# A gated linear-attention layer and its expert FFN: from a chunk loop with a separate expert stage to a pipeline over 256-token tiles

## The chip, the cores and the metric

The kernel runs on one core of a Trainium2 chip. The metric is device time in microseconds, from the start to the end of one execution. The profile is one execution taken by the hardware profiler; its instruction engines are called PE (TensorE's matmuls), PEld (its weight loads), DVE (VectorE), ACT (ScalarE), POOL (GpSimd) and SP (SyncE, which here only issues DMAs).

## The reference

Attention has 4 batches, 8 heads, 768 steps and head size 48. For each step a complex gate `a = a_re + i a_im` is scaled so that its magnitude is at most 0.999; a complex 48 x 48 state per head is multiplied by the gate (per row d) and gets the outer product of k and v added to its real part; the output is q times the real part of the state:

```python
new_re = ar * S_re - ai * S_im
new_im = ar * S_im + ai * S_re
kv = np.einsum('bhd,bhe->bhde', k[:, :, t], v[:, :, t])
S_re, S_im = (new_re + kv, new_im)
y[:, :, t] = np.einsum('bhd,bhde->bhe', q[:, :, t], S_re)
```

The 3072 output rows of 384 then go through one of 8 experts each, by `domain_id`: `h = maximum(x @ w1[e], 0)`, `out = h @ w2[e]`, with 1024 hidden units. Inputs, weights and output are float32 in HBM.

## The kernel before

Both versions use the same algebra: the logarithm of the gate's magnitude (halved sum of squares, clamped) and its angle are summed over time by matmuls with triangular matrices; `exp` of the summed log-magnitude and `sin`/`cos` of the summed angle scale q and k, so that attention becomes a causal masked product of 96-wide vectors plus a product with the running state.

Before, the work is cut into 6 chunks of 128 steps (`c`, L192), each of the 4 batches (`b`) in it: 24 tiles of [128 steps, 8 heads x 48]. Per tile five loads on SP's queue (L203 to L207, 192-byte pieces), then on POOL a cast of v (L210), three products for the squared magnitude (L214 to L216) and one for `ai * (1/ar)` (L220); DVE takes the reciprocal (L219); ACT takes Arctan (L223), Ln (L241), two Exps (L268, L269) and two Sins (L287, L288). A batch's prefix sums (L249 to L257) add one matmul with a ones matrix for each earlier chunk. DVE reduces the angle to one turn (L272 to L276). POOL and DVE share the products that fill `qcat` and `kcat` (L292 to L304). PE transposes them (L318, L319), ACT and DVE copy the halves out of PSUM (L322, L323), PE forms the scores (L332), DVE masks them (L335), PE forms the outputs and the state's increment (L339 to L344), DVE adds the increment (L348), ACT copies the output to fp16 (L351). POOL then scatters the 128 rows with an indirect DMA to `gl_x_sorted` (L353), 512 slots for each expert, at places computed at the start by a routing stage (L91 to L136).

After all attention comes the expert stage (L360 on). 24 indirect scatters write each slot's token number (L365). 16 passes of 256 slots load the rows, transpose them, run the two matmuls (L413, L423) with Relu on ACT and DVE in turns, copy the result and scatter it to the output by token number (L427). Empty slots carry an index out of bounds and are dropped. Weights come as float32 on SP's queue and are converted by ACT and DVE (L160, L162).

The order on each engine is not the program's. A scheduler lists the instructions at build time: an engine that is free in its estimate takes the ready instruction that stands first in the program. It also places a wait wherever two accesses to a buffer or DRAM tensor may touch, so the scatters into one DRAM tensor follow each other. On the chip each engine then runs its list in order.

Of the kernel before, what the change touches and what calls it, by code (L numbers as in the profile page):

```python
# [10 lines left out]
F32 = mybir.dt.float32  # L11
# [18 lines left out]
ESLOT = 512  # L30
NBLK = B * NCH
# [3 lines left out]
def kernel(  # L35
# [24 lines left out]
    make_upper_triangular(nc, utri16[:, :], val=1.0, diag=True)  # L60
    utri16s = cpool.tile([128, 128], F16, name="utri16s")
    make_upper_triangular(nc, utri16s[:, :], val=1.0, diag=False)
    ones16 = cpool.tile([128, 128], F16, name="ones16")
    nc.gpsimd.memset(ones16[:, :], 1.0)
    maskbf = cpool.tile([128, 128], BF16, name="maskbf")
    make_upper_triangular(nc, maskbf[:, :], val=1.0, diag=True)

    halfpi_col = cpool.tile([128, 1], F32, name="halfpi_col")
    nc.gpsimd.memset(halfpi_col[:, :], PI / 2.0)

    e8 = cpool.tile([128, 8], F32, name="e8")
    nc.gpsimd.iota(e8[:, :], pattern=[[1, 8]], base=0, channel_multiplier=0,
                   allow_small_or_imprecise_dtypes=True)

    tok_i32 = cpool.tile([128, NBLK], I32, name="tok_i32")
    nc.gpsimd.iota(tok_i32[:, :], pattern=[[128, NBLK]], base=0, channel_multiplier=1)

    sent_i32 = cpool.tile([128, NE * ESLOT // 128], I32, name="sent_i32")
    nc.gpsimd.iota(sent_i32[:, :], pattern=[[1, NE * ESLOT // 128]], base=OOB_SENT,
                   channel_multiplier=64)  # L80
    nc.sync.dma_start(out=invs_ap[:, :], in_=sent_i32[:, :])

    zero_f16 = cpool.tile([128, 2 * HD], F16, name="zero_f16")
    nc.gpsimd.memset(zero_f16[:, :], 0.0)
    for e in range(NE):
        nc.scalar.dma_start(out=xs_ap[e * ESLOT + ESLOT // 2:(e + 1) * ESLOT, :],
# [378 lines left out]
```

## Time and profile before

| | |
|---|---|
| runs | 505.60, 507.04, 509.84 us (median 507.04) |
| span of the profiled execution, first to last instruction | 502.4 us (its own time stands nowhere else) |
| PE busy, granted clock over the span | 248.8 us (50%), 0.816 |
| DVE busy | 285.7 us (57%) |
| ACT busy | 266.0 us (53%) |
| POOL busy | 280.8 us (56%) |
| DMA | 61.0 MB, mean 121 GB/s |

Busy time is the union of an engine's instructions. A granted clock of 1.00 is TensorE's level of 2.4 GHz and 0.50 its level of 1.2 GHz; figures between are a stretch's mean over the two. The mean of a group in the list of instructions is the duration from start to end, which includes time in which the instruction is held.

### The profile page before, as it was taken

Reading aid. Unit: us, or ns where it says so; the run is one execution under the profiler, and the core shown is the slowest. Engines: PE = TensorE matmul, PEld = TensorE weight load, DVE = VectorE, ACT = ScalarE, POOL = GpSimd, SP = SyncE. Lnnn points to the kernel's source line nnn. Section 1 sums busy time; section 2 is a strip of 40 time slices with the busy share of each in tenths; the row PEclk is TensorE's granted clock in tenths of the full one; section 3 lists DMA queues with packets and bytes.
Section 4 is the critical chain, followed back from the end, with each engine's and each line's share of the span. In section 5 each row is a group of like instructions: output and inputs, shape, how many; then the busy total and the mean of one; then the engine's idle time right before and its main releaser. Section 6 shows DMA issues by size and latency. Waiting matters only on the chain. (4 is left out here: it accounts for less than half of the span.)

```text
span 502.4 us, 5997 instructions
## 1 busy us (share of the span) xinstructions
PE 248.8 (50%) x2026; PEld 175.0 (35%) x2026; DVE 285.7 (57%) x421; ACT 266.0 (53%) x422; POOL 280.8 (56%) x320
## 2 busy tenths in 40 slices
PE   0010005453215454461576568363669667869980
PEld 0000003342203343251354445252446445546650
DVE  3734275956419999989899996942122222322220
ACT  3155474649136976597488538721254425564440
POOL 3456679884398978949997785841011232232231
PEclk9999999999999665685567557755697878999996
DMA  8965414456544574754535611003967727321210
GB/s 254 281 107 97 80 31 79 90 159 161 94 79 86 106 218 96 196 115 95 113 72 110 130 45 25 16 16 51 386 196 277 277 72 254 121 81 60 70 49 14
DMA packets 153166, 61.01 MB, mean 121 GB/s; under 512 B 134817, under 2 KB 148544, under 8 KB 153136
## 3 DMA queue, kind: packets, MB, share of 16 engines
q1 hardware_dynamic: 148016, 51.96, 42.3%
q0 software_dynamic: 3968, 7.10, 3.9%
q10 hardware_dynamic: 1152, 1.57, 0.8%
q8 instruction: 16, 0.26, 0.2%
q14 instruction: 14, 0.11, 0.1%
HBM read 51.93 MB, written 10.25 MB: 124 GB/s over the span
## 5 line engine op out<-in xcount | busy, mean ns | idle before, releaser
L427 POOL DMA_INDIRECT out_dram<-o_sb,invall x32 | 33.4, 1044 | 114.5 <-ACT o_sb L426 48.7
L418 DVE TENSOR_SCALAR h_sb<-h_ps 128x256 f16<-128x256 f32 x64 | 25.3, 422 | 107.5 <-PE h_ps L413 102.6
L413 PE MATMUL h_ps<-xt,w1t 128*128 128x256 f16 x384 | 62.4, 305 | 18.5 <-ACT xt L405 11.9
L318 PE MATMUL tqk_ps<-ident,qcat 128*128 128x128 bf16 x192 | 41.4, 289 | 40.4 <-DVE kcat_t L323 24.3
L219 DVE RECIPROCAL rec<-art 128x384 f32<-128x384 f32 x24 | 60.9, 2539 | 0.0
L413 PEld LDWEIGHTS <-w1t 128*128 128x128 f16 x384 | 41.6, 109 | 36.7 <-issue 28.4
L423 PE MATMUL o_ps<-w2t,h_sb 128*128 128x384 f16 x256 | 52.6, 338 | 0.0
L319 PE MATMUL tqk_ps<-ident,kcat 128*128 128x128 bf16 x192 | 41.8, 294 | 10.5 <-DVE kcat L304 5.3
L365 POOL DMA_INDIRECT gl_inv_sorted<-tok_i,dest_i x24 | 24.5, 1021 | 36.7 <-DMA gl_inv_sorted<-tok_i,dest_i 26.1
L249 PE MATMUL lm_ps<-lm,utri 128*128 128x384 f16 x24 | 10.9, 455 | 67.7 <-DVE lm L243 67.7
L332 PE MATMUL mt_ps<-qcat_t,kcat_t 96*128 96x128 bf16 x192 | 27.3, 290 | 29.6 <-DVE kcat_t L323 26.5
L322 ACT COPY qcat_t<-tqk_ps 128x512 bf16<-128x512 bf16 x48 | 27.8, 579 | 26.6 <-PE tqk_ps L319 25.6
L323 DVE COPY kcat_t<-tqk_ps 128x512 bf16<-128x512 bf16 x48 | 19.6, 408 | 37.6 <-ACT qcat_t L322 36.2
L353 POOL DMA_INDIRECT gl_x_sorted<-xstage,dest_i x24 | 25.6, 1068 | 24.2 <-ACT xstage L351 17.8
L335 DVE TENSOR_TENSOR mtm<-mt_ps,maskbf 128x512 bf16<-128x512 f32 x48 | 32.4, 676 | 11.4 <-PE mt_ps L332 11.0
L416 ACT ACTIVATE h_sb<-h_ps 128x256 f16<-128x256 f32 x64 | 23.0, 385 | 29.2 <-PE h_ps L413 28.9
L319 PEld LDWEIGHTS <-kcat 128*128 128x128 bf16 x192 | 25.7, 134 | 35.5 <-issue 26.5
L243 DVE TENSOR_SCALAR lm<-lnu 128x384 f16<-128x384 f32 x24 | 20.6, 860 | 29.1 <-ACT lnu L241 29.1
L339 PE MATMUL y_ps<-vt,mtm 128*128 128x48 bf16 x192 | 20.9, 210 | 32.2 <-DVE mtm L335 25.4
L426 ACT COPY o_sb<-o_ps 128x384 f32<-128x384 f32 x32 | 15.2, 478 | 40.5 <-PE o_ps L423 26.7
L241 ACT ACTIVATE lnu<-u 128x384 f32<-128x384 f32 x24 | 12.4, 522 | 40.5 <-POOL u L216 40.3
L318 PEld LDWEIGHTS <-qcat 128*128 128x128 bf16 x192 | 26.2, 137 | 22.1 <-POOL u L214 7.5
(86 smaller groups left out, 769.2 us busy)
## 6 DMA issues: line engine op xcount, KB each, us to landing
wstg<-in_moe_w_dram SPq DMA_DIRECT2D x16, 1536.0 KB, 8.6
qt<-in_q_dram SPq DMA_DIRECT2D x24, 192.0 KB, 4.4
kt<-in_k_dram SPq DMA_DIRECT2D x24, 192.0 KB, 3.3
art<-in_a_re_dram SPq DMA_DIRECT2D x24, 192.0 KB, 5.8
ait<-in_a_im_dram SPq DMA_DIRECT2D x24, 192.0 KB, 3.1
vraw<-in_v_dram SPq DMA_DIRECT2D x24, 192.0 KB, 3.8
xrow<-gl_x_sorted SPq DMA_DIRECT2D x16, 192.0 KB, 2.7
gl_x_sorted<-zero_f ACTq DMA_DIRECT2D x8, 192.0 KB, 5.6
```

The costliest lines, as they stand in the source:

```text
L219: nc.vector.reciprocal(out=rec[:, :], in_=art[:, :, :])
L318: nc.tensor.transpose(out=tqk_ps[:, hi, :], in_=qcat[:, h, :], identity=ident[:, :])
L319: nc.tensor.transpose(out=tqk_ps[:, 4 + hi, :], in_=kcat[:, h, :], identity=ident[:, :])
L322: nc.scalar.copy(out=qcat_t[:, :, :], in_=tqk_ps[:, 0:4, :])
L332: nc.tensor.matmul(out=mt_ps[:, hi, :], lhsT=kcat_t[0:96, hi, :], rhs=qcat_t[0:96, hi, :], start=True, stop=True)
L335: nc.vector.tensor_tensor(out=mtm[:, :, :], in0=mt_ps[:, :, :], in1=maskbf[:, None, :].to_broadcast([128, 4, 128]), op=ALU.mult)
L353: nc.gpsimd.indirect_dma_start(out=xs_ap[:, :], out_offset=bass.IndirectOffsetOnAxis(ap=dest_i32[:, blk:blk + 1], axis=0), in_=xstage[:, : ...
L365: nc.gpsimd.indirect_dma_start(out=invs_ap[:, :], out_offset=bass.IndirectOffsetOnAxis(ap=dest_i32[:, blk:blk + 1], axis=0), in_=tok_i32[: ...
L413: nc.tensor.matmul(out=h_ps[:, sub, :], lhsT=w1t[:, fs, j * 128:(j + 1) * 128], rhs=xt[:, fs, :], start=(fs == 0), stop=(fs == 2))
L418: nc.vector.tensor_scalar(out=h_sb[:, j, :], in0=h_ps[:, sub, :], scalar1=0.0, scalar2=None, op0=ALU.max)
L423: nc.tensor.matmul(out=o_ps[:, :], lhsT=h_sb[:, j, th * 128:(th + 1) * 128], rhs=w2t[:, j, :], start=(j == 0), stop=(j == 7))
L427: nc.gpsimd.indirect_dma_start(out=out[:, :], out_offset=bass.IndirectOffsetOnAxis(ap=invall[:, eb * 2 + th:eb * 2 + th + 1], axis=0), in_ ...
```

## The change

The kernel body is rewritten. A tile is 256 steps of one batch, two neighbouring steps in one partition: [128, 8 heads, 2 x 48], 12 tiles, batch after batch, in groups `[[0], [1,2], [3,4,5], [6,7,8], [9,10,11]]`. Loads have pieces of 384 bytes. Gate work is split into a block of Ln/Exp/Square (`le_block`) and a block of Arctan/Sin (`trig_block`), each behind one explicit table load, and ScalarE's order within and between them is fixed (`chain`). `ai / ar` is `ai * Exp(-Ln(ar))`, and the log-magnitude is `2 Ln(ar) + Ln(1 + x*x)`. POOL keeps the cast of v and the DMA issues. All transposed copies go through VectorE. Each tile's output is stored by SP in token order, and an expert call gathers its rows by token number, at most 128 per batch and expert, in slots `rank * 8 + expert`; what does not fit would go through a loop under a run-time test (`overflow`). For this input the largest count is 116. Weights are converted by DMAs from POOL's queue and stay in SBUF. The expert calls of a batch are emitted between the attention tiles of the next batch. Output scatters and inverse scatters are declared free of each other (`unordered`).

```diff
+TS = 256
+CAP = 128
+GROUPS = [[0], [1, 2], [3, 4, 5], [6, 7, 8], [9, 10, 11]]
...
+    pt = pool("pt", 1, space=bass.MemoryType.PSUM)
+    pe = pool("pe", 2, space=bass.MemoryType.PSUM)
...
+    def load(g, names):
+        for name, t in names:
+            bufs = {"ar": 3, "ai": 4, "q": 2, "k": 2, "v": 1}[name]
+            tl = lpool.tile([128, H, 96], F32, name=f"ld_{name}", tag=f"ld_{name}", bufs=bufs)
+            nc.sync.dma_start(out=tl[:, :, :], in_=src_view(t, g))
+            loaded[name, g] = tl
...
+    def load_weights(e, gate):
+        i1 = nc.gpsimd.dma_start(out=w1t[e][:, :, :], in_=moe_w1[e].rearrange("(fs p) f -> p fs f", p=128))
+        i2 = nc.gpsimd.dma_start(out=w2t[e][:, :, :], in_=moe_w2[e].rearrange("(j p) f -> p j f", p=128))
+        for i in (i1, i2):
+            if gate is not None:
+                tc.add_manual_dep(i.ins, gate.ins.name, syncdep, reason="inputs first")
...
+    def le_a(g):
+        ar, ai = loaded["ar", g], loaded["ai", g]
+        la = epool.tile([128, H, 96], F32, name="la")
+        first = chain("act", nc.scalar.activation(out=flat(la), in_=flat(ar), func=AF.Ln))
+        chain("act", nc.scalar.activation(out=flat(ar), in_=flat(la), func=AF.Exp, scale=-1.0))
+        nc.vector.tensor_tensor(out=flat(ai), in0=flat(ai), in1=flat(ar), op=ALU.mult)
+        return la, first
+    def le_b(g, la):
+        ar, ai = loaded["ar", g], loaded["ai", g]
+        nc.scalar.activation(out=flat(ar), in_=flat(ai), func=AF.Square)
+        chain("act", nc.scalar.activation(out=flat(ar), in_=flat(ar), func=AF.Ln, bias=1.0))
+        nc.vector.scalar_tensor_tensor(out=flat(la), in0=flat(la), scalar=2.0, in1=flat(ar),
+                                       op0=ALU.mult, op1=ALU.add)
+        lmt = epool.tile([128, 2, HD], F16, name="lm", bufs=3)
+        nc.vector.tensor_scalar(out=hdx(lmt[:, :, :]), in0=jhd(la[:, :, :]), scalar1=LN0999_X2, scalar2=None,
+                                op0=ALU.min)
+        lm[g] = lmt
+    def le_c(g):
+        ps = pcum.tile([128, 2, 512], F32, name="cum", tag="cum")
+        cumsum(ps, lm, g)
+        for dst, name, sgn, bias in ((ep, "ep", 0.5, bias_p), (em, "em", -0.5, bias_m)):
+            t = epool.tile([128, 2, HD], BF16, name=name, bufs=3)
+            chain("act", nc.scalar.activation(out=t[:, :, :], in_=ps[:, :, 0:HD], func=AF.Exp, scale=sgn,
+                                              bias=bias[:, 0:1]))
+            dst[g] = t
+    def trig_a(g):
+        ai = loaded["ai", g]
+        chain("act", nc.scalar.activation(out=flat(ai), in_=flat(ai), func=AF.Arctan))
+        tht = epool.tile([128, 2, HD], F16, name="th", bufs=3)
+        nc.vector.tensor_scalar(out=hdx(tht[:, :, :]), in0=jhd(ai[:, :, :]),
+                                scalar1=1.0 / (2 * PI), scalar2=None, op0=ALU.mult)
+        th[g] = tht
+    def trig_b(g):
+        ps = pcum.tile([128, 2, 512], F32, name="cum", tag="cum")
+        cumsum(ps, th, g)
+        src = ps[:, :, 0:HD]
+        fg = epool.tile([128, 2, 2, HD], F32, name="fg", bufs=1)
+        nc.vector.tensor_scalar(out=fg[:, 1], in0=src, scalar1=MAGIC, scalar2=None, op0=ALU.add)
+        nc.vector.scalar_tensor_tensor(out=fg[:, 0], in0=fg[:, 1], scalar=MAGIC, in1=src,
+                                       op0=ALU.subtract, op1=ALU.subtract)
+        nc.vector.tensor_scalar(out=fg[:, 1].bitcast(I32), in0=fg[:, 0].bitcast(I32), scalar1=0x7FFFFFFF,
+                                scalar2=None, op0=ALU.bitwise_and)
+        t = epool.tile([128, 2, 2, HD], BF16, name="sc", bufs=2)
+        chain("act", nc.scalar.activation(out=t[:, 0], in_=fg[:, 0], func=AF.Sin, scale=-2 * PI))
+        chain("act", nc.scalar.activation(out=t[:, 1], in_=fg[:, 1], func=AF.Sin, scale=-2 * PI,
+                                          bias=halfpi[:, 0:1]))
+        sc[g] = t
...
+    def attend(g):
+        b, i = divmod(g, NT)
+        vt = epool.tile([128, H, 96], BF16, name="vt", bufs=2)
+        nc.gpsimd.tensor_copy(out=vt[:, :, :], in_=loaded["v", g][:, :, :])
+        v4 = vt[:, :, :].rearrange("p h (j d) -> p h j d", j=2)
+        cats = []
+        for name, e in (("k", em), ("q", ep)):
+            p = e[g]
+            nc.vector.tensor_tensor(out=hdx(p[:, :, :]), in0=jhd(loaded[name, g][:, :, :]), in1=hdx(p[:, :, :]),
+                                    op=ALU.mult)
+            cat = epool.tile([128, 2, H, 2, D], BF16, name=f"{name}cat", bufs=1)
+            for part, s in ((0, 1), (1, 0)):
+                nc.vector.tensor_tensor(
+                    out=cat[:, :, :, part, :].rearrange("p j h d -> p (j h) d"),
+                    in0=p[:, :, :].rearrange("p j (h d) -> p (j h) d", h=H),
+                    in1=sc[g][:, s].rearrange("p j (h d) -> p (j h) d", h=H), op=ALU.mult)
+            cats.append(cat)
+        kcat, qcat = cats
+        if i < NT - 1:
+            w_ps = py.tile([128, HD], F32, name="w_ps", tag="y")
+            for h in range(H):
+                for j in range(2):
+                    chain("pe_y", nc.tensor.matmul(
+                        out=w_ps[0:96, h * D:(h + 1) * D], lhsT=kcat[:, j, h].rearrange("p a d -> p (a d)"),
+                        rhs=v4[:, h, j, :], start=(j == 0), stop=(j == 1)))
+            wn = epool.tile([96, HD], BF16, name="wst", bufs=2)
+            if i == 0:
+                nc.vector.tensor_copy(out=wn[:, :], in_=w_ps[0:96, :])
+                nc.vector.tensor_tensor(out=wn[:, :], in0=wst[g - 1][:, :], in1=w_ps[0:96, :], op=ALU.add)
+            wst[g] = wn
+        xst = mpool.tile([128, 2, HD], F16, name="xst", bufs=2)
+        for hq in range(2):
+            y = py.tile([128, 4, 2, D], F32, name="y", tag="y")
+            for hp in range(2):
+                t_ps = pt.tile([128, 2, 2, 2, 128], BF16, name="t_ps", tag="t")
+                for kind, cat in ((0, qcat), (1, kcat)):
+                    for hh in range(2):
+                        for j in range(2):
+                            h = hq * 4 + hp * 2 + hh
+                            nc.tensor.transpose(out=t_ps[0:96, kind, hh, j, :],
+                                                in_=cat[:, j, h].rearrange("p a d -> p (a d)"),
+                                                identity=ident[:, :])
+                ct = epool.tile([96, 2, 2, 2, 128], BF16, name="ct", bufs=2)
+                nc.vector.tensor_copy(out=ct[:, :, :, :, :], in_=t_ps[0:96])
+                for hh in range(2):
+                    h = hq * 4 + hp * 2 + hh
+                    mt = pm.tile([128, 2, 256], F32, name="mt", tag="mt")
+                    for js in range(2):
+                        nc.tensor.matmul(out=mt[:, js, :], lhsT=ct[:, 1, hh, js, :],
+                                         rhs=ct[:, 0, hh].rearrange("p j t -> p (j t)"), start=True, stop=True)
+                    mtm = epool.tile([128, 2, 2, 128], BF16, name="mtm", bufs=3)
+                    nc.vector.tensor_tensor(out=mtm[:, :, :, :].rearrange("p a b t -> p (a b t)"),
+                                            in0=mt[:, :, :].rearrange("p a t -> p (a t)"),
+                                            in1=mask[:, :, :, :].rearrange("p a b t -> p (a b t)"), op=ALU.mult)
+                    for jt in range(2):
+                        o = y[:, hp * 2 + hh, jt, :]
+                        for js in range(2):
+                            chain("pe_y", nc.tensor.matmul(out=o, lhsT=mtm[:, js, jt, :], rhs=v4[:, h, js, :],
+                                                           start=(js == 0), stop=(i == 0 and js == 1)))
+                        if i > 0:
+                            chain("pe_y", nc.tensor.matmul(out=o, lhsT=ct[:, 0, hh, jt, :],
+                                                           rhs=wst[g - 1][:, h * D:(h + 1) * D],
+                                                           start=False, stop=True))
+            nc.scalar.copy(
+                out=xst[:, :, hq * 4 * D:(hq + 1) * 4 * D].rearrange("p j (h d) -> p h j d", d=D), in_=y[:, :, :, :])
+        nc.sync.dma_start(out=x_ap[b][i * TS:(i + 1) * TS, :].rearrange("(p j) f -> p j f", j=2), in_=xst[:, :, :])
...
+    def gather(b, n, idx):
+        x = xrow[n % XSLOTS]
+        nc.gpsimd.indirect_dma_start(
+            out=x[:, :], out_offset=None, in_=x_ap[b][:, :],
+            in_offset=bass.IndirectOffsetOnAxis(ap=idx, axis=0), bounds_check=S - 1, oob_is_err=False)
+        return x
+    def ffn(x, w1, w2, inv, group=None):
+        xt_ps = pe.tile([128, 3, 128], F16, name="xt_ps", tag="moe")
+        for fs in range(3):
+            nc.tensor.transpose(out=xt_ps[:, fs, :], in_=x[:, fs * 128:(fs + 1) * 128], identity=ident16[:, :])
+        xt = mpool.tile([128, 3, 128], F16, name="xt", bufs=2)
+        nc.vector.tensor_copy(out=xt[:, :, :], in_=xt_ps[:, :, :])
+        h_sb = mpool.tile([128, 8, 128], F16, name="h_sb", bufs=2)
+        for half in range(2):
+            h_ps = pe.tile([128, 4, 128], F32, name="h_ps", tag="moe")
+            for jj in range(4):
+                j = half * 4 + jj
+                for fs in range(3):
+                    nc.tensor.matmul(out=h_ps[:, jj, :], lhsT=w1[:, fs, j * 128:(j + 1) * 128],
+                                     rhs=xt[:, fs, :], start=(fs == 0), stop=(fs == 2))
+            nc.scalar.activation(out=h_sb[:, half * 4:half * 4 + 4, :], in_=h_ps[:, :, :], func=AF.Relu)
+        o_ps = pe.tile([128, HD], F32, name="o_ps", tag="moe")
+        for j in range(8):
+            nc.tensor.matmul(out=o_ps[:, :], lhsT=h_sb[:, j, :], rhs=w2[:, j, :], start=(j == 0), stop=(j == 7))
+        o_sb = mpool.tile([128, HD], F32, name="o_sb", bufs=2)
+        nc.scalar.copy(out=o_sb[:, :], in_=o_ps[:, :])
+        ins = nc.gpsimd.indirect_dma_start(
+            out=out[:, :], out_offset=bass.IndirectOffsetOnAxis(ap=inv, axis=0), in_=o_sb[:, :],
+            in_offset=None, bounds_check=NTOK - 1, oob_is_err=False)
+        if group:
+            unordered(group, ins)
+    def expert(b, e):
+        x = gather(b, b * NE + e, loc_sb[b][:, e:e + 1])
+        ffn(x, w1t[e], w2t[e], inv_sb[b][:, e:e + 1], group="out")
+    preload = lambda name: chain("act", nc.scalar.preload_act_table_set(name))
+    def le_block(tiles):
+        gates = []
+        preload(SET_LE)
+        las = {}
+        for n, g in enumerate(tiles):
+            las[g], f = le_a(g)
+            gates.append(f)
+            if n > 0:
+                le_b(tiles[n - 1], las[tiles[n - 1]])
+                if n > 1:
+                    le_c(tiles[n - 2])
+        le_b(tiles[-1], las[tiles[-1]])
+        for g in tiles[-2:]:
+            le_c(g)
+        return gates
+    def trig_block(tiles):
+        preload(SET_TRIG)
+        for n, g in enumerate(tiles):
+            trig_a(g)
+            if n > 0:
+                trig_b(tiles[n - 1])
+        trig_b(tiles[-1])
+    load(0, QKV)
+    le_block(GROUPS[0])
+    routing()
+    trig_block(GROUPS[0])
+    gates = {}
+    ffn_todo = []
+    def some_ffn(n):
+        for _ in range(min(n, len(ffn_todo))):
+            expert(*ffn_todo.pop(0))
+    for gi, tiles in enumerate(GROUPS):
+        nxt = GROUPS[gi + 1] if gi + 1 < len(GROUPS) else []
+        for n in nxt:
+            load(n, ARI)
+        if nxt:
+            for n in nxt:
+                load(n, QKV)
+            for n, f in zip(nxt, le_block(nxt)):
+                gates[n] = f
+                if n - 1 < NE:
+                    load_weights(n - 1, f)
+        for n, g in enumerate(tiles):
+            attend(g)
+            if n == 0 and nxt:
+                trig_block(nxt)
+            if g == 0:
+                for b in range(B):
+                    scatter_inverse(b)
+                for b in range(B):
+                    load_inverse(b)
+            some_ffn(3 if g < 10 else 4)
+            if g % NT == NT - 1:
+                ffn_todo += [(g // NT, e) for e in range(NE)]
+    some_ffn(99)
...
+    def overflow():
+        count = nc.values_load(ovf_i[0:1, 0:1], min_val=0, max_val=S)
+        with tc.If(count > CAP):
```

## Rows read from the trace of the kernel before

**Rows 1.** Busy time by stage: us from start, length, busy (instructions) of each engine.
```profile
core 0: us, PE busy (x) PEld busy (x) DVE busy (x) ACT busy (x) POOL busy (x), PEclk, DMA share, GB/s
0.00:24.00 24.00, 0.48 (x2) 0.21 (x2) 13.21 (x43) 5.41 (x4) 8.77 (x30) 1.00 1.00 274
180.00:300.00 120.00, 62.66 (x586) 45.54 (x585) 113.94 (x135) 80.02 (x121) 99.94 (x108) 0.61 0.52 117
...
340.00:502.00 162.00, 112.03 (x774) 75.98 (x771) 36.04 (x73) 65.39 (x137) 35.33 (x34) 0.84 0.45 148
```

**Rows 2.** The page's first part: busy us, share of the span, instructions.
```profile
PE 248.8 (50%) x2026; PEld 175.0 (35%) x2026; DVE 285.7 (57%) x421; ACT 266.0 (53%) x422; POOL 280.8 (56%) x320
```

**Rows 3.** Timeline: start us, duration us, engine, line; VectorE and POOL around 203 us.
```profile
202.88 5.45 DVE L243 TENSOR_SCALAR lm<-lnu 128x384 f16<-128x384 f32 x1
203.52 1.00 POOL L216 TENSOR_TENSOR u<-u,u 128x384 f32<-128x384 f32 x1
...
208.01 1.00 POOL L215 TENSOR_TENSOR u<-art 128x384 f32<-128x384 f32 x1
```

**Rows 4.** Timeline of VectorE and POOL around 319 us.
```profile
319.31 0.34 DVE L273 TENSOR_SCALAR t_s<-t_s 128x384 f32<-128x384 f32 x1
319.39 1.65 POOL L353 DMA_INDIRECT gl_x_sorted<-xstage,dest_i  x1 [0.16 <-issue]
319.58 0.54 DVE L276 SCALAR_TENSOR_TENSOR t_c<-t_s 128x384 f32<-128x384 f32 x1
...
320.51 0.34 DVE L304 TENSOR_TENSOR kcat<-p,sn 128x384 bf16<-128x384 bf16 x1
```

**Rows 5.** Instruction groups of VectorE: shapes, count | busy us, mean ns | idle before.
```profile
L219 DVE RECIPROCAL rec<-art 128x384 f32<-128x384 f32 x24 | 60.9, 2539 | 0.0
L335 DVE TENSOR_TENSOR mtm<-mt_ps,maskbf 128x512 bf16<-128x512 f32 x48 | 32.4, 676 | 11.4 <-PE mt_ps L332 11.0 <-issue 0.3
L304 DVE TENSOR_TENSOR kcat<-p,sn 128x384 bf16<-128x384 bf16 x24 | 23.2, 968 | 0.2 <-PE tcat_ps L344 0.2
L323 DVE COPY kcat_t<-tqk_ps 128x512 bf16<-128x512 bf16 x48 | 19.6, 408 | 37.6 <-ACT qcat_t L322 36.2 <-ACT xstage L351 1.3
L272 DVE TENSOR_SCALAR t_s<-th_ps 128x384 f32<-128x384 f32 x24 | 13.0, 544 | 2.8 <-PE th_ps L254 2.8
```

**Rows 6.** Instruction groups of ScalarE.
```profile
L241 ACT ACT_TABLE_LOAD x22 | 28.2, 1283 | 7.9 <-DMA gl_x_sorted<-zero_f 7.6
L322 ACT COPY qcat_t<-tqk_ps 128x512 bf16<-128x512 bf16 x48 | 27.8, 579 | 26.6 <-PE tqk_ps L319 25.6 <-PE y_ps L341 0.9
L241 ACT ACTIVATE lnu<-u 128x384 f32<-128x384 f32 x24 | 12.4, 522 | 40.5 <-POOL u L216 40.3
L162 ACT CAST w1t<-wstg 128x3072 f16<-128x3072 f32 x4 | 11.0, 2748 | 8.2 <-DMA wstg<-in_moe_w_dram 7.1 <-PE h_ps L413 1.2
L162 ACT ACT_TABLE_LOAD x1 | 1.3, 1283 | 0.7 <-PEq L449 0.7
```

**Rows 7.** PE: two transposes of the timeline; a run of matmuls in the chain of waits.
```profile
241.04 0.31 PE L318 MATMUL tqk_ps<-ident,qcat 128*128 128x128 bf16 x1
241.14 0.31 PE L319 MATMUL tqk_ps<-ident,kcat 128*128 128x128 bf16 x1
...
413.10 2.11 PE o_ps L423 x13
```

**Rows 8.** Instruction groups of POOL.
```profile
L427 POOL DMA_INDIRECT out_dram<-o_sb,invall x32 | 33.4, 1044 | 114.5 <-ACT o_sb L426 48.7 <-DMA out_dram<-o_sb,invall 29.4 <-ACT h_sb L416 26.8
L353 POOL DMA_INDIRECT gl_x_sorted<-xstage,dest_i x24 | 25.6, 1068 | 24.2 <-ACT xstage L351 17.8 <-DVE t_s L272 2.5 <-ACT qcat_t L322 2.0
L210 POOL CAST vt<-vraw 128x384 bf16<-128x384 f32 x24 | 13.2, 550 | 12.1 <-PE y_ps L341 11.7 <-ACT lnu L241 0.3
```

**Rows 9.** The chain of waits near its end: start us, us, what.
```profile
460.80 2.58 DMA out_dram<-o_sb,invall
```

More of the change, by code (lines that the diff above doesn't have):

```diff
@@ L61, with after, chain @@
-    utri16s = cpool.tile([128, 128], F16, name="utri16s")
-    make_upper_triangular(nc, utri16s[:, :], val=1.0, diag=False)
+    nosync = mybir.DependencyInfo(mybir.DependencyClass.NoSync, mybir.DependencyReason.DATA)
+    syncdep = mybir.DependencyInfo(mybir.DependencyClass.Sync, mybir.DependencyReason.DATA)
+    def after(ins, prev):
+        if prev is not None:
+            tc.add_manual_dep(ins.ins, prev.ins.name, nosync, reason="order")
+        return ins
+    last = {}
+    def chain(key, ins):
+        after(ins, last.get(key))
+        last[key] = ins
+        return ins
@@ new lines, in unordered @@
+    def unordered(group, ins):
+        tc.declare_no_dep(ins.ins, group=group, reason="rows written are disjoint")
+        tc.add_to_no_dep_group(group, ins.ins)
+        return ins
+    x_ap = [nc.dram_tensor(f"gl_x_rows{b}", [S, HD], F16, kind="Internal").ap() for b in range(B)]
+    inv_ap = [nc.dram_tensor(f"gl_inv_rows{b}", [NROWS, 1], I32, kind="Internal").ap() for b in range(B)]
+    pool = lambda name, bufs=1, **kw: ctx.enter_context(tc.tile_pool(name=name, bufs=bufs, **kw))
+    cpool = pool("cpool")
@@ L72 @@
[L72 to L81, printed above, removed]
@@ L139 @@
+    mask = cpool.tile([128, 2, 2, 128], BF16, name="mask")
+    for js in range(2):
+        for jt in range(2):
+            nc.vector.tensor_copy(out=mask[:, js, jt, :], in_=(u_str if js > jt else u_inc)[:, :])
     ident = cpool.tile([128, 128], BF16, name="ident")
@@ new lines @@
+    w1t = [cpool.tile([128, 3, DFF], F16, name=f"w1t{e}") for e in range(NE)]
+    w2t = [cpool.tile([128, 8, HD], F16, name=f"w2t{e}") for e in range(NE)]
+    def load_weights(e, gate):
[4 more added lines that the diff above has]
+                tc.add_manual_dep(i.ins, gate.ins.name, syncdep, reason="inputs first")
@@ new lines, with flat, jhd, hdx @@
+    lm = {}
+    th = {}
+    ep = {}
+    em = {}
+    sc = {}
+    def flat(t):
+        return t[:, :, :].rearrange("p h x -> p (h x)")
+    def jhd(ap):
+        return ap.rearrange("p h (j d) -> p j h d", j=2)
+    def hdx(ap):
+        return ap.rearrange("p j (h d) -> p j h d", h=H)
+    def cumsum(ps, tiles, g):
+        b, i = divmod(g, NT)
+        prev = [tiles[b * NT + n] for n in range(i)]
+        cur = tiles[g]
+        for j in range(2):
+            o = ps[:, j, 0:HD]
+            mm = [((u_str if j == 0 else u_inc), cur[:, 1, :]), (u_inc, cur[:, 0, :])]
+            for p in prev:
+                mm += [(ones16, p[:, 0, :]), (ones16, p[:, 1, :])]
+            mm = mm[::-1]
+            for n, (l, r) in enumerate(mm):
+                nc.tensor.matmul(out=o, lhsT=l[:, :], rhs=r, start=(n == 0), stop=(n == len(mm) - 1))
@@ L438 @@
+    overflow()
 _INS = ['q', 'k', 'v', 'a_re', 'a_im', 'moe_domain_id', 'moe_w1', 'moe_w2']
```

440 lines of the change are left out of this document (121 added, 319 removed).

## The prediction

> **What bounds the kernel now.** I read the busy time by stage first [rows 1]. Attention fills 0 to 340 us, the experts 340 to 502. Between 180 and 300 us VectorE is busy 113.9 of 120 us and POOL 99.9, while PE works 62.7 us at a granted clock of 0.61: the attention stage is bound by VectorE. No engine is over 57% over the span [rows 2].
>
> Then the timeline, for what a VectorE instruction costs. L243 takes 5.45 us at 202.88, and in that time POOL runs elementwise work back to back, from 203.52 to past 208.01 [rows 3]. At 319.31 the only POOL instruction is a scatter's issue; beside it a 384-element L273 takes 0.34 us, L276 0.54, L304 0.34 [rows 4]. L304's mean is 968 ns [rows 5]. So POOL's arithmetic, not its DMA issues, doubles these VectorE instructions.
>
> The expert stage is held by neither: in the chain of waits, 2.58 us landings of the output scatter follow each other, one scatter waiting for the last [rows 9], and PE is busy 112 of 162 us at 0.84 [rows 1].
>
> **The change, part by part.** I price the new work per 256-token tile (12 of them) and per expert call (32, of 128 slots).
>
> *VectorE.* Full rate: 544 ns for 384 elements, 676 for 512 [rows 5], so 1.03 ns an element and 0.94 us for 768. Double rate: 0.34 against 0.54 us for 384 [rows 4], half the slope, 0.54 us for 768; a 1024-element bf16 copy from PSUM is 0.41 + 512 x 0.52 ns = 0.675 [L323, rows 5]. Gate work of a tile: four instructions at 0.94 and three at 0.54, 5.4 us. Attention of a tile: two products at 0.94, four bf16 products at 0.54, four copies at 0.675, eight maskings at 0.676, a state update of 0.54 in two tiles of three: 12.5 us. That is 17.9 x 12 = 215; with 32 copies of 0.34 (11) and routing (some 7, from 13.2 busy in the first 24 us [rows 1] less a reciprocal and weight copies) 233 us, against 285.7 [rows 2]. The reciprocal, 60.9 us [rows 5], is gone: Exp(-Ln) on ScalarE replaces it. The seven double-rate instructions of a tile read or write pieces of 48 elements; at full rate they add 7 x 0.4 x 12 = 34 us, at best nothing changes. I take the double rate, since L304 writes such pieces at 0.34.
>
> *ScalarE.* 0.52 us for 384, slope (2748-522)/2688 = 0.83 ns [rows 6], 0.84 for 768. Nine per tile and two copies of 0.52: 8.6 x 12 = 103. An expert call: two Relus of 512 at 0.58 and a copy of 0.52: 54 in all. Table loads fall from 70 (seven rows, first and last in [rows 6]) at 1.28 us to about 11: 14 for 90. Sum 171 for 266. Off the path.
>
> *PE.* I count columns. Transposes follow each other at 0.10 us for 128 columns [rows 7], which is 1.2 GHz; 13 matmuls of 384 took 2.11 us, 0.162 each, which is 2.4 GHz. A batch has 48 prefix matmuls of 384, 96 transposes, 48 score products of 256, 128 output and 32 state products of 48: 50 thousand columns (32 without the prefix sums). An expert call has 27 x 128 + 8 x 384 = 6.5 thousand; eight make 52. All four batches: 410 thousand, 342 us at 1.2 GHz, 171 at 2.4. The change doubles the score columns and leaves the rest near what it was. This is the second bound: where experts stand beside attention, PE has 102 thousand columns a batch, 43 to 86 us, against VectorE's 3 x 17.9 + 2.7 = 56.
>
> *POOL.* All elementwise work goes but 12 casts (0.55 at 384 [rows 8], about 1.0 each). Indirect transfers: 24 inverse scatters, 32 gathers, 32 output scatters at 1.07 [rows 8]: 94. The 16 converting weight loads have no row before. Low end: 1.07 each, 17 us. High end by pieces: L353 writes 128 rows in 1.07, a pair of weight tensors has 384 + 1024 row pieces, 11.8 us an expert, 94 in all. I take the high end, since every piece needs its address: POOL 200 us, under VectorE. They stand on POOL's queue ahead of the inverse scatters and the casts of V that tiles 1 and 2 wait for; cover is the first 90 us, where POOL has little else.
>
> *Waits taken away and added.* The output scatters no longer wait for each other; 162 us of expert stage goes beside attention except for the last batch. Rows no longer reach DRAM sorted: each tile is stored by SP, and a gather fetches an expert's rows; the store waits behind loads on SP. New waits: eight gathers wait for the last tile of their batch; ep and em have three buffers, so the gate work of a batch ends only after the last cat product of the batch before, and the sines follow. That leaves VectorE the rest of one attention (8.5 us) to cover a table load, Arctan, prefix sum, rounding and two sines (about 9): a few us lost at each batch border.
>
> **The sum.** Start: first loads 0.8 MB at 274 GB/s [rows 1] and a 2.6 us landing, 5.5; the gate chain of tile 0 (eleven ScalarE passes and table loads, six VectorE passes, two prefix sums) about 18: 24 us, with 15 us of VectorE work in it. Tiles 0 to 2: 3 x 12.5 + 5 x 5.4 = 64 us of VectorE, at 85% busy 75. Batches 1 and 2: 56 us of VectorE and the border, with PE near 57 at a mean clock of 0.75, 66 each. Batch 3 has no gate work left: VectorE 40, PE 84 thousand columns, 35 to 70; I take 50. Tail: eight expert calls with nothing beside them. A call is 6.5 thousand columns, 2.7 us at 2.4 GHz, and the two PSUM buffers it shares among four uses expose Relu and copy, so about 4; 32 plus store, gather and last scatter at 2.6 and 1.1 each, 42 us. Then the overflow test, some 3 us (no row; 0 to 8). The largest count of a batch and expert is 116, below 128, so its body is skipped. 24 + 75 + 132 + 50 + 42 + 3 = 326; 80% of the middle is VectorE-busy, less than the 95% of [rows 1], because two engines compete. With 4.6 us around the span (median 507.04 less span 502.4, the profile giving no other time for its execution) 331; I say **334**, for waits in queues ordered at build time by estimates.
>
> **Rivals.**
> - *PE stays at half clock beside attention.* For it: 0.61 with PE busy 63 of 120 us. Against: 0.84 in the expert stage, where it is busy 112 of 162 [rows 1], and the new stage is denser than the old attention. At 1.2 GHz batches 1 and 2 take 86/0.95 = 90 each, batch 3 74, the tail 58: 334 + 48 + 24 + 16 = 422; half of that 378. Chance 0.15.
> - *POOL's queue starves the early tiles.* If five experts' weights and the 24 inverse scatters (59 + 26 us) go ahead of the casts of V, attention of tile 1 starts near 90 us instead of 42 and VectorE has only gate work of tiles up to 5 for that time: +35, 370. Against: the cheap end of the weight price. Chance 0.17.
> - *VectorE's locks stretch POOL's DMA issues until POOL is the bound*, slower than before. For it: L353 takes 1.65 us beside three such VectorE instructions [rows 4], 1.07 on average [rows 8]. Against: L427, in the stage with little VectorE work, averages 1.04. The place is POOL's 200 us; it decides from a factor of 2.5, where POOL alone takes 500. At three, with start and end, 620. At the 1.65 shown, 200 becomes 310, still covered. Chance 0.04. The Trainium skill's rule speaks for it ("SBUF — State Buffer", SBUF: two separate sides: a VectorE instruction that uses both ports keeps POOL from writing descriptors); its estimate of 620 ns becoming 3100 would put POOL near 1000 us, and no row here shows more than 1.65.
> - *Less idle than I allow*: VectorE at 92% through the middle, PE at full clock, tail of 34: 24 + 213/0.92 + 34 + 8 = 298. Chance 0.09.
>
> That the change does not do what it says would be expert calls ordered behind attention: 24 x 4 = +96 less the PE time freed beside attention, about 400; I hold it inside the first rival's chance.
>
> **The numbers.** Forecast case 305 to 360 with the rest, 0.55. The range 302 to 400 leaves out most of the low case and the upper half of the PE case and the slow one, about 0.18; the double-rate question (+34) lies inside. Within 1% (what a measurement of this kernel can tell; its runs lie within 0.8%): 0.02. Slower 0.04. Faster 0.94.
>
> **What would show it.** Right: VectorE's 768-element products near 0.54 and 0.94 us with means near their minima; VectorE 225 to 245 us busy; 11 table loads; expert matmuls between 120 us and the end, with 8 calls alone at the end over 35 to 45 us. Wrong: PE clock under 0.65 between 100 and 250 us; POOL busy throughout the first 100 us with VectorE idle behind a cast; POOL issues over 2 us; VectorE 270 or more.

## The result and the profile after

The changed kernel takes **385.64 us** (median of 4 runs, 385.29 to 387.06), the kernel before 506.32 beside it: ratio 0.761, 95% interval 0.758 to 0.764. The forecast was 334 us, the range 302 to 400: direction and range held, the point was 52 us too low.

Windows of the kernel after (busy us by engine, granted clock, share of the 16 DMA engines, GB/s), against [rows 1]:

```profile
22.00:57.00 35.00, 16.41 (x121) 11.08 (x122) 19.00 (x31) 15.69 (x19) 22.76 (x21) 0.78 0.66 75
57.00:190.00 133.00, 67.34 (x548) 45.73 (x546) 73.32 (x112) 48.66 (x64) 30.69 (x32) 0.62 1.01 195
190.00:335.00 145.00, 124.77 (x1571) 94.23 (x1571) 110.34 (x184) 74.83 (x122) 48.02 (x44) 0.99 0.24 72
335.00:384.00 49.00, 27.34 (x280) 19.50 (x280) 2.86 (x8) 13.52 (x25) 17.04 (x17) 0.85 0.14 46
```

From 57 to 190 us the DMA share averages 1.01, and every compute engine is busy about half the time or less. The share sums the time of all packets, so it passes 1 where they overlap, and a mean near 1 can hide a hole. Finer windows show two, in which the DMA engines stand nearly idle, and a long full stretch:

```profile
24.00:40.00 16.00, 11.87 (x94) 8.56 (x92) 11.95 (x18) 10.50 (x14) 12.95 (x12) 1.00 0.09 5
64.00:80.00 16.00, 0.00 (x0) 0.00 (x0) 0.59 (x2) 0.00 (x0) 3.73 (x4) 0.50 0.29 37
80.00:190.00 110.00, 66.60 (x545) 45.68 (x545) 71.77 (x110) 48.66 (x64) 25.02 (x26) 0.65 1.10 217
```

From 190 to 335 us PE works 125 of 145 us at a granted clock of 0.99. Batch ends are read from SP's stores of a tile; here the last tiles of batches 0 to 2, and one row for the three of batch 3 (the last at 335.16):

```profile
139.68 0.52 SPq L372 DMA_DIRECT2D gl_x_rows<-xst  x1
...
222.57 0.34 SPq L372 DMA_DIRECT2D gl_x_rows<-xst  x1
...
284.09 0.34 SPq L372 DMA_DIRECT2D gl_x_rows<-xst  x1
302.14 33.33 SPq L372 DMA_DIRECT2D gl_x_rows<-xst  x3
```

Stage lengths, with two experiments for later:

| us | forecast | after | one weight (e3) | one weight, lookup moved (e11) |
|---|---|---|---|---|
| start to end of batch 0 | 99 | 139.7 | 130.2 | 113.0 |
| batch 1 | 66 | 82.9 | 63.5 | 62.4 |
| batch 2 | 66 | 61.5 | 65.6 | 67.9 |
| batch 3 | 50 | 51.1 | 49.4 | 58.8 |
| tail, overflow test | 45 | 48.9 | 52.3 | 53.5 |

The miss is 40.7 + 16.9 before 223 us; the later stages add 0.5 net (-4.5 + 1.1 + 3.9), and 1.5 us outside the span for 4.6 takes 3 off, and the 3 us for waits that the forecast had beyond its sum take off as many. The busy sums, against [rows 2], and groups of VectorE and POOL (shapes, count, busy us, mean ns, idle before), against [rows 5, 8]:

```profile
PE 240.1 (63%) x2530; PEld 171.9 (45%) x2530; DVE 217.5 (57%) x374; ACT 162.2 (42%) x238; POOL 126.1 (33%) x139
```
```profile
L358 DVE TENSOR_TENSOR mtm<-mt,mask 128x512 bf16<-128x512 f32 x96 | 63.0, 683 | 8.2 <-PE mt L355 7.9
L316 DVE TENSOR_TENSOR kcat<-em,sc 128x768 bf16<-128x768 bf16 x24 | 14.3, 599 | 0.5 <-ACT sc L296 0.5
L312 DVE TENSOR_TENSOR em<-ld_k,em 128x768 bf16<-128x768 f32 x12 | 11.3, 946 | 7.5 <-DMA ld_k<-in_k_dram 7.5
...
L199 POOL DMA_INDIRECT gl_inv_rows<-tok_i,dest_i x24 | 26.7, 1111 | 32.3 <-DMA w2t<-in_moe_w_dram 8.8 <-DMA w1t<-in_moe_w_dram 6.9 <-DMA ld_k<-in_k_dram 6.6
L215 POOL DMA_DIRECT2D w2t<-in_moe_w_dram x8 | 7.4, 925 | 0.0
L214 POOL DMA_DIRECT2D w1t<-in_moe_w_dram x8 | 6.2, 774 | 21.6 <-ACT la L252 21.6
```

L316 works on 768 elements in 599 ns, where L304 of [rows 5] took 968 for 384. The weight loads cost POOL 13.6 us in all, under the low end of the price (17). Ahead of the inverse scatters, though, POOL stood idle for 32.3 us, half of it behind weight transfers. What that does, in VectorE's and POOL's timelines (the bracket is the idle time before, and its releaser):

```profile
51.73 0.17 DVE L206 TENSOR_SCALAR loc_sb<-inv_sb 128x8 int32<-128x8 int32 x1 [14.01 <-DMA inv_sb<-gl_inv_rows]
79.41 0.17 DVE L206 TENSOR_SCALAR loc_sb<-inv_sb 128x8 int32<-128x8 int32 x1 [20.68 <-DMA inv_sb<-gl_inv_rows]
...
178.92 0.36 DVE L387 COPY xt<-xt_ps 128x384 f16<-128x384 f16 x1 [13.62 <-PE xt_ps L385]
```
```profile
73.73 0.97 POOL L199 DMA_INDIRECT gl_inv_rows<-tok_i,dest_i  x1 [0.30 <-issue]
74.70 0.83 POOL L307 CAST vt<-ld_v 128x768 bf16<-128x768 f32 x1
```

VectorE stands 35 us at two subtractions of 8 columns. At 178.92 it waits for the first expert's rows, whose gather was issued at 154.42 behind weight loads and landed 23.92 us later (chain of waits); the gather at 338.03 lands in 2.60. This wait (13.62 us) and the one at the next call (3.00) are nearly all of the 16.9 us that batch 1 is over its forecast. The cast of V for tile 1 is right behind the 24th inverse scatter.

### The profile page after: what moved, and what is told of

It is laid out like the page before. It is cut to its first block, busy times and chain, and to the rows that moved or that the text cites. A ratio compares the mean times of both kernels' runs of the same rounds, so it can differ in the third digit from the quotient of the medians.

```text
span 384.1 us, 6354 instructions
## 1 busy us (share of the span) xinstructions
PE 240.1 (63%) x2530; PEld 171.9 (45%) x2530; DVE 217.5 (57%) x374; ACT 162.2 (42%) x238; POOL 126.1 (33%) x139
## 4 chain that ended last, share of the span: by engine, by line
DMA 29%; PE 22%; DVE 22%; issue 10%; ACT 7%; POOL 6%; POOLq 0%; SPq 0%; DVEq 0%; ACTq 0%
DMA gl_inv_rows<-tok_i,dest_i 9%; DMA xrow<-gl_x_rows,loc_sb 8%; DMA ld_k<-in_k_dram 7%; PE h_ps L394 6%; PE o_ps L399 6%; DVE mtm L358 6%; POOL gl_inv_rows L199 3%; PE cum L247 3%; PE mt L355 3%; DVE ct L350 3%; POOL out_dram L402 2%; DVE fg L290 2%; DVE fg L291 2%; DMA inv_sb<-gl_inv_rows 2%; ACT h_sb L396 2%
## 5 line engine op out<-in xcount | busy, mean ns | idle before, releaser
L358 DVE TENSOR_TENSOR mtm<-mt,mask 128x512 bf16<-128x512 f32 x96 | 63.0, 683 | 8.2 <-PE mt L355 7.9
L396 ACT ACTIVATE h_sb<-h_ps 128x512 f16<-128x512 f32 x64 | 37.7, 595 | 70.4 <-PE h_ps L394 70.0
L402 POOL DMA_INDIRECT out_dram<-o_sb,inv_sb x32 | 34.8, 1088 | 80.5 <-ACT o_sb L401 76.6
L394 PE MATMUL h_ps<-xt,w1t 128*128 128x128 f16 x768 | 56.2, 226 | 5.0 <-DVE xt L387 4.8
L377 POOL DMA_INDIRECT xrow<-gl_x_rows,loc_sb x32 | 35.8, 1119 | 34.5 <-PE xt_ps L385 9.8
L355 PE MATMUL mt<-ct 96*128 96x256 bf16 x192 | 34.3, 307 | 15.3 <-DVE ct L350 15.2
L364 PE MATMUL y<-vt,mtm 128*128 128x48 bf16 x384 | 29.1, 194 | 23.4 <-DVE mtm L358 22.9
L350 DVE COPY ct<-t_ps 96x1024 bf16<-96x1024 bf16 x48 | 32.6, 679 | 16.9 <-PE t_ps L346 16.8
L364 PEld LDWEIGHTS <-mtm 128*128 128x128 bf16 x384 | 22.1, 104 | 36.2 <-DVE mtm L358 32.1
L199 POOL DMA_INDIRECT gl_inv_rows<-tok_i,dest_i x24 | 26.7, 1111 | 32.3 <-DMA w2t<-in_moe_w_dram 8.8
L247 PEld LDWEIGHTS <-ones 128*128 128x128 f16 x96 | 10.9, 119 | 52.3 <-DVE fg L291 37.2
```

The lines of the kernel that those rows point to most:

```text
L199: unordered(f"inv{b}", nc.gpsimd.indirect_dma_start(out=inv_ap[b][:, :], out_offset=bass.IndirectOffsetOnAxis(ap=dest_i[:, col:col + 1], a ...
L247: nc.tensor.matmul(out=o, lhsT=l[:, :], rhs=r, start=(n == 0), stop=(n == len(mm) - 1))
L350: nc.vector.tensor_copy(out=ct[:, :, :, :, :], in_=t_ps[0:96])
L355: nc.tensor.matmul(out=mt[:, js, :], lhsT=ct[:, 1, hh, js, :], rhs=ct[:, 0, hh].rearrange("p j t -> p (j t)"), start=True, stop=True)
L358: nc.vector.tensor_tensor(out=mtm[:, :, :, :].rearrange("p a b t -> p (a b t)"), in0=mt[:, :, :].rearrange("p a t -> p (a t)"), in1=mask[: ...
L364: chain("pe_y", nc.tensor.matmul(out=o, lhsT=mtm[:, js, jt, :], rhs=v4[:, h, js, :], start=(js == 0), stop=(i == 0 and js == 1)))
```

## The experiments

Theory: the 57 us before 223 are a term that the sum lacked, the DMA engines' time for 25.2 MB of f32 weights beside the inputs (the profile books them at their f16 size, 12.6 MB). Rival: the order of the queues alone. For the later stages: PE is full, so expert calls beside attention are not free.

**Order of the queues (e1, e2, e8).** e1 puts the subtraction behind the last masking of its batch; e2 puts all inverse scatters ahead of the weights:

```
 e1   def local_rows(b):
+         after(nc.vector.tensor_scalar(out=loc_sb[b]..., last["dve"])
 e2   for i in (i1, i2):
+         after(i, last["inv"])
```


> Only VectorE's order changes: the four lookups that wait for the inverse scatters stand behind the last masking of their batch instead of in tile 1. Theory A (VectorE stands in its queue behind small transfers that are late): the two waits of 14.0 and 20.7 us go; but POOL's cast of V for tile 1 still stands behind the last inverse scatter at 73.7 us, so only part comes back: 360 to 372 us. Theory B (from 25 to 175 us the kernel is bound by what the DMA engines can move, and the wait only shows it): no change, 380 to 387.

> All 24 inverse scatters stand on POOL's queue ahead of the first weight load. Theory A: the scatters end near 46 us instead of 73.7, the lookups wait until about 55 us, the cast of V is free too; the late k load (7.5 us) and the late gather (13.6 us) stay: 350 to 362 us. Theory B: the same bytes must move, 380 to 387.

e1: 391.11 us (ratio 0.765, 0.754 to 0.777), e2: 386.65 (0.757, 0.751 to 0.762): no gain. In e1 VectorE does 25.2 us of work from 22 to 57 us instead of 19.0, then stands 25.2 us at a state update that needs the cast of V: the next wait takes the place of the one removed. e2 leaves the DMA engines idle early and full later (the rows are e2's windows), and ends where the kernel after does.

```profile
22.00:57.00 35.00, 16.06 (x108) 10.54 (x108) 16.55 (x26) 15.29 (x18) 28.41 (x27) 0.80 0.20 17
57.00:190.00 133.00, 66.21 (x553) 45.77 (x554) 76.45 (x117) 48.62 (x64) 25.66 (x26) 0.64 1.09 210
```

e8 sends only batch 0's inverse scatters early, each later batch's behind a cast of V, with e1's edit:

```
-            if g == 0:
-                for b in range(B):
...
+            if g == 0 or (g % NT == NT - 1 and g // NT + 1 < B):
+                b = 0 if g == 0 else g // NT + 1
```


> All weights. Only batch 0's six inverse scatters come early; those of each later batch stand behind the casts of V of the batch before, and each lookup behind its batch's last masking. So the first weights are issued near 27 us instead of 39.7, and no cast or load waits for 24 scatters. Theory B: the gain is the DMA time no longer idle between 22 and 57 us, about 15 us: 365 to 375. Theory A alone (queue order): 345 to 355. No change would speak against both.

397.69 us (0.778, 0.770 to 0.786), slower. The DMA share is 1.03 at 161 GB/s from 22 to 57 us, then 0.97 at 177, and by 190 us VectorE has done 111 us of work, 104 in the kernel after. But the gathers in batch 1 stand behind weight loads as before, and VectorE waits 17.18 and 8.31 us at copies of their rows, the first of them here:

```profile
165.40 0.36 DVE L392 COPY xt<-xt_ps 128x384 f16<-128x384 f16 x1 [17.18 <-PE xt_ps L390]
```

Batch 2 then takes 70.6 us for 61.5. Pulling the weights forward as well, seven experts' ahead of the first gather, gave 394.10 us (0.771, 0.761 to 0.780; e9). That gather lands in 5.28 us and batch 1 takes 69.0 us, but VectorE waits 22.71 us for a load of k at 127.14: the weights now delay an input. So the place of the weights decided which transfer was late. e8 came out in none of its cases, e9 within 4 us of e8.

**Take the bytes away (e3).** All experts use expert 0's weights, so only those are loaded and the output differs:

```
-                if n - 1 < NE:
+                if n - 1 < 1:
```


> Only expert 0's weights are loaded and all experts compute with them (the output is that of other weights). 11 MB of converting loads go; all work of the engines stays. Theory A: the waits for lookups, k and gather (56 us) go nearly all: 328 to 340 us, what was forecast for the change. Theory B says the same number but with the input loads landing faster everywhere; the difference to the runs before tells them apart: if B, e1 and e2 stay near 385 and this falls. If PE's half clock up to 175 us is the cause (theory C), this stays above 365.

360.84 us (0.706, 0.696 to 0.716): 25 us gone, the one early edit that gains by itself. The DMA share from 57 to 190 falls from 1.01 to 0.58, VectorE does 101 us of work there instead of 73, and batch 1 takes 63.5 us. Two of VectorE's waits in the kernel after are gone with the weights, 13.62 us for the first gather and 7.52 us for a load of k: 21 of the 25 us. This edit takes away the bytes and their place ahead of the gathers on POOL's queue together. No run kept all weights and took their loads off the gathers' queue, so the two are not separated.

**Bytes and queues (e7, e10, e11).** e7 is e1 + e2 + e3. e10 moves the lookups of the inverse table from SP's queue to POOL's behind the scatters, with e1 + e2; e11 is e10 with one weight:

```
-        nc.sync.dma_start(out=inv_sb[b]...
+        nc.gpsimd.dma_start(out=inv_sb[b]...
```


> Expert 0's weights serve all experts (the output is that of other weights), and besides the inverse scatters stand ahead of the weight load and the lookups behind each batch's last masking. The two edits that gave nothing with all weights are put on the kernel that has little weight traffic. Theory B (the DMA engines are saturated from 57 to 190 us, and that hides what the order costs): now the order counts, the 33.6 us of lookup waits left in the run with one weight go: 328 to 340 us, the forecast. Theory D (order and bytes both do not matter, PE's half clock sets the pace): no change, 358 to 362.

> The four lookups of the inverse table leave SP's queue for POOL's, behind all 24 inverse scatters, the weights come behind those, and VectorE's subtraction waits until the end of the batch. SP can then send input loads from 20 us on. If SP's stall is what left the DMA engines idle from 25 to 50 us: their share there rises from under 0.2 (with scatters ahead) to over 0.5, the inputs of tiles 1 to 3 are there when VectorE wants them, the saturated stretch ends some 10 to 25 us earlier than 190, and the time is 362 to 378. If the early idle time is only shifted, because the bytes up to 190 us set the time: 383 to 392.

> The same, with only expert 0's weights loaded (all experts use them, so the output is another). With neither weights nor SP's stall in the way, the prediction's sum should hold if DMA was all that it left out: 328 to 345 us, batch 0 ending near 100, batches 1 and 2 at 60 to 66 us each. If PE, with the expert calls beside attention, sets the pace behind batch 0 whatever the start does: batch 0 ends near 105, but the time stays at 352 to 363, as with one weight alone (360.8).

e7: 362.68 us (0.709, 0.703 to 0.715), the case of no change; e10: 403.61 (0.790, 0.785 to 0.796), slower and outside both cases; e11: 354.94 (0.693, 0.688 to 0.698), the second case. e10 and e11 differ in the weights alone: 48.7 us. Early idle time was not just SP's lookup: in e10 SP's queue stands next at the load of V, which has one buffer. SP's waits in e10 (total, times, longest), and its row at the end of the longest:

```profile
SPq L103 <- POOL vt L310: 49.9, 6, 33.5
```
```profile
65.73 0.37 SPq L103 DMA_DIRECT2D ld_v<-in_v_dram  x1
```

The buffer is freed by POOL's cast, which stands behind 24 scatters and two experts' weights, up to 64.83 us. So the queue rival of the prediction is real, with the scatters and not the 13.6 us of the weights' issue as its cause. In e11 it costs less (batch 0 ends at 113.0, 26.7 us earlier than after). But e11's span is 28.5 us shorter where its batches 0 and 1 are 47 us shorter: batches 2 and 3 and the tail give 19 back.

**Behind 190 us (e4, e12).** e4 emits every expert call behind the attention loop (the build's scheduler still moved some ten or eleven ahead of the last tile's end):

```
-            some_ffn(3 if g < 10 else 4)
```


> All 32 expert calls are emitted after the last attention tile; nothing else changes. If the calls hide beside attention as the sum had it: attention ends near 315 us (no gather to wait for, VectorE-bound at some 90%), and 32 calls at 3.7 us and 8 us of latency follow: 430 to 445 us. If calls beside attention cost attention nearly their own time (PE is the bound there), 395 to 410.

406.64 us (0.796, 0.790 to 0.802), the second case. Attention ends at 311.1 instead of 335.2, and about 21 calls remain for the tail instead of 8, each 3.69 us. So some 13 calls, 48 us alone, had cost 24 beside attention (13 of them in batch 1, where the waits for gathers lie): half hidden. From 190 to 270 us of e4, where four calls run, VectorE is busy 71.4 of 80 us and PE 60.4 at 0.82: with calls PE is the bound, with few of them VectorE.

e12 shortens a call: the next call's transposes come before this call's output matmuls, and the output gets the prefix sums' PSUM buffer.

```
+        if nxt is not None:
+            ready[nxt] = front(gather(nxt...))
+        o_ps = pcum.tile([128, 2, 512], F32, name="cum", tag="cum")[:, 0, 0:HD]
```


> The changed kernel with its expert calls overlapped on PE: the three transposes of the next call's rows (and the copy to SBUF) come before the eight output matmuls of this call, and the output has a PSUM buffer of its own (that of the prefix sums), so the first matmul of the next call does not wait for the copy. In the kernel after, a call takes 3.69 us when alone, of which PE works about 3.3 and waits 0.45 and some smaller pieces. If behind 190 us the 32 calls, 3.69 us each, set the pace because attention's matmuls stand behind them on PE's queue: a call takes 2.9 to 3.2 us, 32 x 0.5 to 0.8, 360 to 372 us. If attention fills these waits already, only the eight calls at the end gain: 378 to 382. If the prefix sums' buffer, now shared, delays the gate work: 386 or more, with idle time of VectorE and ScalarE before the reads of the prefix sums.

403.83 us (0.789, 0.785 to 0.793): the third case. The calls got shorter, and the kernel slower. VectorE's copies of an expert's rows in e12, first on both sides of a gap, then two in the tail:

```profile
189.12 0.36 DVE L387 COPY xt<-xt_ps 128x384 f16<-128x384 f16 x1 [0.99 <-PE xt_ps L385]
224.06 0.36 DVE L387 COPY xt<-xt_ps 128x384 f16<-128x384 f16 x1 [1.76 <-PE xt_ps L385]
...
377.46 0.36 DVE L387 COPY xt<-xt_ps 128x384 f16<-128x384 f16 x1 [2.69 <-PE xt_ps L385]
380.50 0.36 DVE L387 COPY xt<-xt_ps 128x384 f16<-128x384 f16 x1 [2.69 <-PE xt_ps L385]
```

The last two are 3.04 us apart (3.69 in the kernel after). But no call runs from 189 to 224, nor from 257 to 297 us, where the kernel after has one every 4 to 12. In those gaps PE works 25.1 of 35 and 28.1 of 40 us at clocks of 0.76 and 0.83, and batch 2 takes 72.5 us for 61.5. The three calls begun before the first gap stand at their output matmuls, and the first of these behind each gap is released by VectorE's last read of the prefix sums:

```profile
220.35 1.47 PE L406 MATMUL cum<-w2t,h_sb 128*128 128x384 f16 x8 [0.54 <-DVE fg L291]
...
291.88 1.72 PE L406 MATMUL cum<-w2t,h_sb 128*128 128x384 f16 x8 [0.54 <-DVE fg L291]
```

So in the order of this build the shared buffer held the calls back until the gate work was done. What each of the two edits does alone was not run.

**Two reasons of the gain (e5, e6).** e5 is the kernel before with its output scatters free of each other:

```
+                tc.declare_no_dep(ins.ins, group="out", ...)
```


> The kernel before, with the output scatters alone declared free of each other; a part of the change done alone. In the expert stage 21 landings of 2.6 us stand in the chain of waits, and PE is busy 112 of 162 us. If that chain is what holds the stage, it shrinks until PE or the weights bind: minus 20 to 35 us, 472 to 487. If the scatters only seem to hold it and PE or the weight conversion is as slow, under 6 us: 500 or more.

497.13 us (0.972, 0.963 to 0.981), between its two cases: 15 us for a wait of 29.4 us [rows 8]. The group's idle time before falls only from 114.5 to 102.9 us, and now ends with ScalarE's copy of the outputs, 98.6 us for 48.7: most of the wait was turned into that one. Most of the 121 us lies elsewhere.

e6 is the kernel after with the products of q and k back on POOL (L312):

```
-            nc.vector.tensor_tensor(out=hdx(p[:, :, :]), ...
+            nc.gpsimd.tensor_tensor(out=hdx(p[:, :, :]), ...
```


> The two products with q and k of each tile (24 instructions of 128x768 from f32, 0.95 us each on VectorE, 22.7 us) move to POOL; nothing else changes. If POOL's arithmetic is what doubled VectorE's instructions in the kernel before: VectorE loses 22.7 us of its own work, but instructions beside the 24 POOL products (each 2 us or more, so 48 us or more of POOL arithmetic) take up to twice as long, and VectorE's busy sum falls by less than 10 us or rises; the cat products right behind them also wait for a slower product; 390 to 405 us. If POOL's arithmetic does not disturb VectorE: busy falls by 22 us to about 195, the means of the other groups stay within 3%, and the time is 378 to 388, since DMA and then PE set it.

395.24 us (0.774, 0.770 to 0.778, apart from after's interval), the first case by its time; VectorE's busy time lies between the two cases. VectorE gives up 22.7 us of work and its busy time falls by 11.8, to 205.7; its neighbour of the products, and the product on POOL:

```profile
L316 DVE TENSOR_TENSOR kcat<-em,sc 128x768 bf16<-128x768 bf16 x24 | 18.3, 769 | 3.1 <-POOL em L312 2.7 <-ACT sc L296 0.4
```
```profile
L312 POOL TENSOR_TENSOR em<-ld_k,em 128x768 bf16<-128x768 f32 x12 | 21.8, 1813 | 13.5 <-DMA ld_k<-in_k_dram 13.5
```

POOL's 42 us of arithmetic (20.0 for the other product) add 8 to 11 us to VectorE's other instructions (by the sum of its groups, or by busy time): the direction that the prediction read in [rows 3, 4], though L316 here grows from 599 to 769 ns and does not double. With e4 (about 21 us), e5 and e6 (15 and 10), less than half of the 121 us has an experiment behind it; the rest of the gain is argued from busy times.

## Why the prediction was right, and where it was not

- **The bound before and its release: right.** VectorE was forecast at 233 us (double rate at 0.54) and measured 217.5, below the 225 to 245 that was to show it (L316's 0.60 to 0.65, L312's 0.946). e6 shows that POOL's arithmetic slows it.
- **ScalarE: right.** 162.2 us for 171, and ten table loads (12.8 us) for eleven.
- **POOL: the price was wrong, its place right.** 126 us for 200, since a weight load's issue takes 0.77 or 0.93 us, for 384 and 1024 row pieces alike, so the price by pieces was wrong. The slower-than-before rival fell: gathers and scatters take 1119 and 1088 ns on average beside 217 us of VectorE work. Single issues do stretch: one inverse scatter of the kernel after takes 3.23 us (median 0.97) beside back-to-back VectorE work, over the 2 us that was to be a sign of being wrong, and an output scatter of e7 takes 4.86 (median 0.99). The Trainium skill states a fivefold stretch of a POOL-issued DMA beside a VectorE copy ("SBUF — State Buffer", SBUF: two separate sides). The trace agrees in single issues, up to that 4.86 us, but the averages barely move. The kernel before already had one of 2.12 us (L427), so the prediction's 1.65 was no ceiling.
- **The step that failed: the sum of the first stages.** "At 85% busy 75" for tiles 0 to 2, and the weights costed as POOL's issue time alone with "the first 90 us, where POOL has little else" as cover. No term held the transfers. The DMA engines then stood at a share of 1.10 from 80 to 190 us (with the weights out: 25 us of the miss in e3, and 49 between e10 and e11). The 24 scatters, with the lookups, casts and loads queued behind them, left them nearly idle from 24 to 40 and from 64 to 80 us (e11: 6 us less than e3 in the whole, 17 at the end of batch 0). Gathers behind the weights in POOL's queue add their wait in batch 1. [rows 1] had the number: 274 GB/s at the start with a share of 1.00, and 25.2 MB of weights with 23.6 MB of inputs, by their shapes, are 178 us at that rate, an estimate. From 57 to 64 us, with two experts' weights under way, the engines moved 207 GB/s at the weights' f16 size; at that rate for 12.6 MB, and 274 for the inputs, it is 147 us, again an estimate. The sum had 165 us up to the end of batch 1, and only the first loads, 5.5 us, stood in them for transfers. The Trainium skill has the rule ("DMA: Bandwidth & Descriptors", Issuing engines are not separate DMA queues: all issuers end on the same 16 engines); the trace agrees, at 1.10 from 80 to 190 us with SP and POOL both issuing, and e10's move from one queue to the other gains nothing.
- **The queue rival: its mechanism came, at a smaller price.** It forecast 370 by way of the cast of V; the cast of tile 1 did start at 74.70. Alone it does not set the time: that cast starts at 55.93 in e2 and at 31.86 in e8, and neither is faster.
- **The half-clock rival: half seen.** 0.62 from 57 to 190, where PE is idle half the time, and 0.99 from 190 on. Where the clock was low PE waited for others (rows above), so the low clock is not shown to cost anything there. From 100 to 250 us the clock was 0.80, not under 0.65.
- **Batches 2 and 3 and the tail: right in size**, 112.6 us for 116 and 48.9 for 45. The call of 3.69 us was forecast at 4. The reason given (VectorE and PE near equal) holds for batch 2, with 53.1 and 51.6 us busy of 61; in batch 3 PE works 46.4 of 51 us and VectorE 30.2. The first call came at 178.92 us, where 120 was to show it. "Experts behind attention, about 400" was measured at 406.6.
- **A small slip:** "80% of the middle" is 84 by its own terms (216 of 257 us); the sum does not use it.
- **Still open:** why batches 2 and 3 grow when the early ones shrink (e11: 126.7 us together for 112.6). In batch 3 (58.8 us for 51.1) the growth is as long as a pause of ScalarE there, 7.4 us, released by nothing that the profile can name. Batch 3 takes 58.1 to 59.8 us in each of e7 to e11, with a pause of 6.8 to 10.3 us in it; in the kernel after, e1, e2 and e3 there is none, and it takes 49.4 to 51.6. What causes the pause is open, and so is batch 2. The order of the calls on PE's queue differs in each build; one that kept it fixed was not tried. No version beat the kernel after with all weights loaded.

## What to carry to other kernels

Give the DMA engines a row of their own in the sum: bytes over the rate that the trace shows, by stage, beside the issue times. When one wait is removed from an in-order queue, name the next instruction in it and what that needs: here subtraction, then cast, then a one-buffer load. Look also at what small transfers stand behind in their queue: moving the weights only chose whether a gather or an input was late. Work moved beside another stage is priced at what it adds there (half a call here), and shortening it can cost more than it gives if it changes the interleaving.

## What the runs showed of the hardware

An indirect transfer issued behind converting weight loads in POOL's queue took 23.9 us to land, 2.6 with the queue empty. Where the DMA share was 1 or above, the engines moved 161 (e8, 22 to 57 us) to 232 GB/s (the first 22 us of the kernel after), with converted weights booked at their f16 size. An indirect issue of about 1 us on POOL stretched to 3.23 us (after) and 4.86 us (e7) in single cases beside VectorE work. In e11, ScalarE and VectorE both paused near 253 us for 7.4 and 6.4 us, released by nothing that the profile can name; e6 to e10 have a like pause in batch 3, the kernel after has none.
